# Attention, routed experts and a second network on one core: the cross products of split operands go from float32r to bfloat16

## The chip, the cores and the metric

The kernel runs on one core of one Trainium2 chip. Its time is the time on the device, in microseconds (us), from launch to end; 825.88 us is the median of three executions before the change. Less is better.

## The reference

Three stages feed each other. Everything is float32 at the interface.

```python
# 1. attention over B, H, S, D = 4, 8, 576, 64, plus a memory term
a = softmax(q @ k.T / 8, causal);  local = a @ v
mem = (phi(q) @ M_prev) / (phi(q) @ z_prev + 1e-6)      # phi(x) = max(x, 0) + exp(min(x, 0))
x = (sig(beta) * mem + (1 - sig(beta)) * local)         # 2304 tokens of 512
# 2. routing: each token goes to one of 8 experts, 288 tokens each, greedily by score
order = argsort(-(x @ w_gate).flatten())                # first come, first served
out[tokens of e] = maximum(x[tokens of e] @ w1[e], 0) @ w2[e]       # 512 -> 1024 -> 512
# 3. the second network, on all tokens
h = maximum(maximum(x @ w1, x @ w2), x @ w3);  y = h @ w_out        # 512 -> 768 -> 512
```

## The kernel before

**Attention** (`attention`) works through 16 pairs of heads. While it runs, 24 tiles of the second network's weights are loaded and turned into float32, and the first four of twelve blocks of 1024 columns are split in two parts (lines 976 to 995). It ends with the gate's scores in `L` and the 2304 rows of x in DRAM.

**Routing** (`routing`) takes eight rounds, one per expert. A round finds the expert that fills next by a search with thresholds: VectorE writes 0/1 flags into a tile `cq` (line 1140), TensorE counts them with tiny bfloat16 matmuls (line 1148), VectorE narrows the interval, and so on. Then VectorE and TensorE turn the round's 288 tokens into a list of indices (lines 1211 to 1225): `cq` holds one-hot rows of 96 columns, and line 1219 uses all its 128 columns as weights. Columns 32 to 127 of `cq` are set to zero once by GpSimd (line 1062), since the first round fills only part of them. The first round is the only one with nothing else to do on TensorE; 88 dummy matmuls on `ones` (line 1310) are spread over its end.

**Experts and second network** (`experts`) go through the eight experts in the order in which routing finds them. For expert p: gather 288 rows of x (three indirect DMAs of GpSimd), transpose them, then for each of 8 weight blocks `fb` the first product h1 (16 groups of matmuls into the PSUM tile `w`), ReLU, and the second product y (into four PSUM tiles `acc`). The second network follows for the same 288 tokens: six feature blocks of three products each (p stage, line 1523 on), maximum over the three, and the output product o on chunks of 128 tokens, with 512 columns. So each matmul of h1, y and p moves 288 columns, and each of o moves 512.

**Split operands.** Every operand of these products is kept in two float32r parts: `hi`, the value rounded to float32r, and `lo`, what is left. The helper `mm3` issues three matmuls per product:

```python
nc.tensor.matmul(o, wh, rh, start=start, stop=False)    # line 1430
nc.tensor.matmul(o, wh, rl, start=False, stop=False)    # line 1431
nc.tensor.matmul(o, wl, rh, start=False, stop=stop)     # line 1432
```

ScalarE makes `hi` (lines 1282, 1321, 1377 and the helper `copy`, line 1268), VectorE makes `lo` by a subtraction (lines 1295, 1327, 1329, 1383). `W32` are the second network's float32 weights, `mh` and `ml` their parts, `wraw`, `whi`, `wlo` those of an expert, `hh` and `hl` the hidden layer's, `gf`/`gc` the maximum's. Blocks 4 and 5 of `ml` are made by another way: ScalarE writes minus `mh`, and a DMA adds `W32` to it (lines 1286 and 1289).

**What sets the order.** Each engine executes its instructions in one fixed order. `Plan` builds that order when the kernel is built: a task has a key (due time), a cost per engine and dependencies, and a list scheduler places them. Keys and costs are the numbers in `RKEY`, `R1KEY`, `FK` and in the `add` calls. So a changed key moves instructions on all engines.

Of the kernel before, what the change touches and what calls it, by code (L numbers as in the profile page):

```python
# [17 lines left out]
try:  # L18
# [4 lines left out]
F32 = mybir.dt.float32  # L23
# [22 lines left out]
RKEY = (-1000, -66.2)  # L46
FL0 = 3
NFILL = 88
R1, R1KEY = 9, 28.8
NK, KD = 4, 6  # L50
# [4 lines left out]
         "mt": 2, "ob": 3, "gc": 7, "gf": 2}  # L55
FK = {"m2": -600, "ml": 28.3, "load": -59.9, "w2": -3.8, "wsplit": -31.9, "gather": -128.4, "xt": -126.2, "h1": 0, "y": 4.0, "o": 12.0, "store": 68.8, "idx": -41.0}
# [185 lines left out]
def attention(g, tc, ctx, consts, beta, qN, kN, v1, vT, mz, mT, wg, xd, L, m2):  # L242
# [738 lines left out]
    for k in range(NK):  # L981
# [6 lines left out]
        def fl(e, k=k, a=0):  # L988
            if a == 0:
                g.slot(k)  # L990
            V.tensor_sub(g.ML[k][:, a:a + 512], g.W32[k][:, a:a + 512], g.MH[k][:, a:a + 512].bitcast(F32))
# [3 lines left out]
        low = add(n + .2, {"DVE": dve(512)}, lambda e, fl=fl: fl(e, a=512), [low])  # L995
    emit(tc, plan)
# [45 lines left out]
def routing(g, tc, plan, rt, rps, L):  # L1042
# [19 lines left out]
    plan.op(-600, {"POOL": 800}, lambda e: nc.gpsimd.memset(cq[:, :, 32:], 0.0), (), [f"cq{a}" for a in range(0, NB, CQ[0])])  # L1062
# [59 lines left out]
    for ph in range(E):  # L1122
# [87 lines left out]
        for a in range(0, NB, q):  # L1210
# [6 lines left out]
            def idx(a0=a + q - w, w=w):  # L1217
# [3 lines left out]
            r.ti = P((30 if ph else 70) * w + (60 if ph else 0), idx, " ".join(f"cq{x}" for x in range(a + q - w, a + q, q)) + " mov0 mov1 mov2" +  # L1221
# [26 lines left out]
def experts(g, tc, plan, top, wr, xd, idxd, out):  # L1248
# [12 lines left out]
    def act(n):  # L1261
        return 35 + 0.89 * n
# [13 lines left out]
    def msub(t, i, c, n):  # L1276
        return t[3 * i + c // 1024][:, c % 1024:c % 1024 + n]

    low = None
    for k in range(NK, 12):  # L1280
# [3 lines left out]
        def fneg(e, k=k):  # L1284
            g.slot(k)
            A.mul(ML[k], MH[k].bitcast(F32), -1.0)

        def facc(e, k=k):
            G.dma_start(ML[k].bitcast(F32), g.W32[k], accum_op=OP.add)

        def flow(e, k=k, h=0):
# [3 lines left out]
            V.tensor_sub(ML[k][:, q], g.W32[k][:, q], MH[k][:, q].bitcast(F32))  # L1295
# [403 lines left out]
```

## Time and profile before

| what | value |
|---|---|
| median of three executions | 825.88 us (824.94 to 826.33) |
| the profiled execution, its own time | 824.29 us |
| its span, first to last instruction | 822.2 us |
| granted TensorE clock, mean of the span | 0.981 of 2.4 GHz |
| TensorE busy | 789.6 us, 96% |
| VectorE, ScalarE, GpSimd busy | 560.3, 355.9, 109.0 us |
| attention, about | 0 to 242 us |
| first routing round and first gather, about | 242 to 276 us |
| experts and second network, about | 276 to 815 us |

The profiled execution is 1.59 us below the median of the three. Matmuls are pipelined, and the record of one is much longer than the distance to the next; so the distance between the starts of two matmuls is read, not the length of a record. The same holds on the other engines, to a lesser degree.

### The profile page before, as it was taken

How to read it: one execution, taken by the hardware profiler on the slowest of the kernel's cores; microseconds unless marked ns; L12 is line 12 of the kernel's file. 1: busy time of each engine (PE TensorE's matmuls, PEld its weight loads, DVE VectorE, ACT ScalarE, POOL GpSimd, SP SyncE). 2: the span in 40 equal slices, each digit the busy share in tenths (PEclk: the TensorE clock that was granted, in tenths of full speed). 3: DMA queues.
4: the chain of work that ended last, by engine and by line, in shares of the span. 5: the costliest groups of instructions: out<-in, count | busy, mean ns of one | idle time of the engine just before them, and what ended most of it. 6: DMA issues, size and time to landing. Idle time of an engine off the chain costs nothing.

```text
span 822.2 us, 18334 instructions
## 1 busy us (share of the span) xinstructions
PE 789.6 (96%) x7022; PEld 745.9 (91%) x7022; DVE 560.3 (68%) x1687; ACT 355.9 (43%) x941; POOL 109.0 (13%) x242
## 2 busy tenths in 40 slices
PE   8999999999974899999999999999999999999996
PEld 6898999999974899999999999989999999999995
DVE  7799999999456996896677576575667643533321
ACT  4668776767645431344234235224313423423311
POOL 2212222223112100301020011011002011001001
PEclk9999999999995899999999999999999999999999
DMA  8364747565015412344033015004303621521000
GB/s 243 90 222 144 242 125 246 165 208 165 23 59 103 146 53 78 119 129 145 2 108 127 27 43 192 27 14 157 103 2 109 138 44 66 142 24 52 1 2 39
DMA packets 39534, 84.82 MB, mean 103 GB/s; under 512 B 11486, under 2 KB 14230, under 8 KB 39446
## 3 DMA queue, kind: packets, MB, share of 16 engines
q1 hardware_dynamic: 35574, 72.87, 29.0%
q0 software_dynamic: 3872, 10.78, 4.6%
q8 instruction: 55, 0.90, 0.5%
q14 instruction: 33, 0.27, 0.1%
HBM read 72.77 MB, written 9.74 MB: 100 GB/s over the span
## 4 chain that ended last, share of the span: by engine, by line
PE 77%; issue 11%; DVE 7%; DMA 2%; POOL 1%; ACT 1%; SPq 0%; DVEq 0%; POOLq 0%; ACTq 0%
PE w L1430 12%; PE w L1431 12%; PE w L1432 12%; PE av L684 9%; PE acc L1430 6%; PE acc L1431 6%; PE acc L1432 6%; PE st L643 5%; PE rps L590 2%; PE rps L1148 2%; DVE junk L456 2%; PE rps L543 1%; PE w L1407 1%; PE st L443 1%; DMA QN<-in_qN 1%
## 5 line engine op out<-in xcount | busy, mean ns | idle before, releaser
L1430 PE MATMUL w<-yh,mh 128*128 128x288 f32 x576 | 172.1, 299 | 0.0
L1431 PE MATMUL w<-yl,mh 128*128 128x288 f32 x576 | 170.3, 296 | 0.0
L1432 PE MATMUL w<-yh,ml 128*128 128x288 f32 x576 | 169.5, 294 | 0.0
L1431 PEld LDWEIGHTS w<-yl,mh 128*128 128x128 f32 x576 | 108.3, 188 | 1.8
L1430 PEld LDWEIGHTS w<-yh,mh 128*128 128x128 f32 x576 | 108.2, 188 | 1.9
L1432 PEld LDWEIGHTS w<-yh,ml 128*128 128x128 f32 x576 | 108.3, 188 | 0.0
L684 PE MATMUL av<-V,pt 128*128 128x112 f32 (+1 forms) x960 | 105.3, 261 | 1.7 <-issue 0.6
L684 PEld LDWEIGHTS av<-V,pt 128*128 128x128 f32 (+1 forms) x960 | 97.0, 173 | 6.4 <-issue 2.3
L1383 DVE TENSOR_TENSOR wlo<-wraw,whi 128x512 fp32r<-128x512 f32 x128 | 84.3, 685 | 13.7 <-ACT whi L1377 13.5
L1537 DVE TENSOR_TENSOR mt<-w,mt 128x288 f32<-128x288 f32 x96 | 43.7, 455 | 61.7 <-PE w L1432 61.1
L1377 ACT CAST whi<-wraw 128x512 fp32r<-128x512 f32 x128 | 73.2, 620 | 21.8 <-DMA wraw<-in_wr 11.4
L1430 PE MATMUL w<-xhi,whi 128*128 128x288 f32 x256 | 77.3, 302 | 0.7 <-DVE xlo L1329 0.7
L1268 ACT CAST gc<-mt 128x64 fp32r<-128x64 f32 (+2 forms) x72 | 17.4, 245 | 138.3 <-DVE mt L1537 111.4
L1430 PE MATMUL acc<-hh,whi 128*128 128x288 f32 x256 | 76.5, 299 | 0.0
L1431 PE MATMUL w<-xlo,whi 128*128 128x288 f32 x256 | 76.1, 297 | 0.0
L1432 PE MATMUL w<-xhi,wlo 128*128 128x288 f32 x256 | 75.9, 296 | 0.0
L1431 PE MATMUL acc<-hl,whi 128*128 128x288 f32 x256 | 75.4, 294 | 0.0
L1432 PE MATMUL acc<-hh,wlo 128*128 128x288 f32 x256 | 75.1, 293 | 0.0
L456 DVE CUSTOM_DVE_ANT_0 junk<-st,mask 128x512 bf16<-128x512 f32 (+3 forms) x128 | 62.5, 488 | 15.6 <-ACT pt L668 4.0
L1321 ACT ACTIVATE hh<-w 128x288 fp32r<-128x288 f32 x64 | 26.3, 411 | 92.9 <-PE w L1432 87.1
L1327 DVE SCALAR_TENSOR_TENSOR hl<-w,hh 128x288 fp32r<-128x288 f32 x64 | 29.1, 455 | 47.3 <-ACT hh L1321 46.7
L670 ACT ACTIVATE pt<-st 128x512 f32<-128x512 f32 x96 | 53.3, 601 | 16.2 <-PE st L643 15.9
(272 smaller groups left out, 1706.7 us busy)
## 6 DMA issues: line engine op xcount, KB each, us to landing
wraw<-in_wr SPq DMA_DIRECT2D x64, 512.0 KB, 3.8
m2raw<-in_m2w SPq DMA_DIRECT2D x12, 512.0 KB, 5.5
V<-in_v SPq DMA_DIRECT2D x16, 365.0 KB, 4.9
KR<-in_kN SPq DMA_DIRECT2D x16, 288.0 KB, 3.1
QN<-in_qN SPq DMA_DIRECT2D x16, 288.0 KB, 3.3
vt<-in_vT SPq DMA_DIRECT2D x16, 288.0 KB, 5.3
xd<-x SPq DMA_DIRECT2D x16, 256.0 KB, 2.9
m2raw<-in_m2w SPq DMA_DIRECT2D x12, 256.0 KB, 3.2
```

The source lines that it names most:

```text
L456: V.tensor_tensor_reduce(out=junk[:, :w], in0=o.s[x][:, c:c + w], in1=m, scale=1.0, scalar=-3.0e38, op0=OP.add, op1=OP.max, accum_out=r.nm ...
L643: PE.matmul(d[:kr, c:c + z - a], neg[q, :kr] if wt is None else wt[q, k], mv[q, a:z], start=x == 0, stop=x == 3)
L670: A.activation(r.PT[:, i, 512 * gi:512 * gi + 512], o.t[i], AF.Exp, scale=0.125)
L684: PE.matmul(AV[:m, i, j * C:j * C + w], r.PT[:, i, o:o + m], r.V[:, c:c + w], start=kb == 0, stop=kb == j)
L1321: A.activation(hi(), src(), AF.Relu)
L1327: V.scalar_tensor_tensor(lo(), src(), 0.0, hi().bitcast(F32), op0=OP.max, op1=OP.subtract)
L1377: A.copy(x.W[fb][0][:, q], x.RAW[fb][:, q])
L1383: V.tensor_sub(x.W[fb][1][:, q], x.RAW[fb][:, q], x.W[fb][0][:, q].bitcast(F32))
L1430: nc.tensor.matmul(o, wh, rh, start=start, stop=False)
L1431: nc.tensor.matmul(o, wh, rl, start=False, stop=False)
L1432: nc.tensor.matmul(o, wl, rh, start=False, stop=stop)
L1537: V.tensor_max(q.mt, o.pt[:, :T], q.mt)
```

## The change

1. **The two cross products on bfloat16.** `lo` becomes a bfloat16 tile with two planes: plane 0 is the rest as before, rounded to bfloat16, and plane 1 is `hi` rounded to bfloat16. `mm3` keeps the first matmul in float32r and does the other two on bfloat16 parts. The tiles have the same size in bytes.
2. **One more instruction per split** makes plane 1: on ScalarE for weights (`wlo`, `ml`), on ScalarE or VectorE for the rest, as the scheduler finds better. `hi` of an operand that isn't ReLU may now also be made by VectorE.
3. **Finer tasks where stages change**: the last block of y and the first product of p are two tasks each, first the float32r matmuls, then the bfloat16 ones.
4. **No clearing of `cq`** (line 1062 is gone); line 1219 in the first round uses 96 of its columns instead of 128.
5. **Blocks 4 and 5 of `ml`** are made like the others; the two DMAs go.
6. New keys and costs.

```diff
-RKEY = (-1000, -66.2)
+RKEY = (-1000, -23.5)
-R1, R1KEY = 9, 28.8
-NK, KD = 4, 6
+R1, R1KEY = 9, 21.8
+NK = 4
...
         low = add(n + .2, {"DVE": dve(512)}, lambda e, fl=fl: fl(e, a=512), [low])
+        low = add(n + .3, {"ACT": act(1024)}, lambda e, k=k: A.copy(g.ML[k][:, 1], g.MH[k].bitcast(F32)), [low])
...
-    plan.op(-600, {"POOL": 800}, lambda e: nc.gpsimd.memset(cq[:, :, 32:], 0.0), (), [f"cq{a}" for a in range(0, NB, CQ[0])])
...
-                    nc.tensor.matmul(IX, cq[:, x], mov[:, x], start=(x == 0), stop=(x == NB - 1))
+                    nc.tensor.matmul(IX[:z], cq[:, x, :z], mov[:, x], start=(x == 0), stop=(x == NB - 1))
...
-        if k < KD:
-            low = add(FK["m2"] + k + .1, {"ACT": act(1024)}, fneg, [t, low])
-            low = add(FK["m2"] + k + .2, {"POOL": 1100}, facc, [low], lat=11000)
-        else:
-            for h in range(2):
-                low = add(FK["ml"] + .1 * k + .05 * h, {"DVE": dve(512)}, lambda e, f=flow, h=h: f(e, h=h), [t, low, g.rounds[0].tt])
+        for h in range(2):
+            low = add(FK["ml"] + .1 * k + .05 * h, {"DVE": dve(512)}, lambda e, f=flow, h=h: f(e, h=h), [t, low, g.rounds[0].tt])
+        low = add(FK["ml"] + .1 * k + .07, {"ACT": act(1024)}, lambda e, k=k: A.copy(ML[k][:, 1], MH[k].bitcast(F32)), [low])
...
-        t = add(key, {"ACT": act(n)}, f1, dep, new=new, use=use)
-        return t, add(key + .01, {"DVE": dve(n)}, f2, [t] + list(dep), use=list(new) + list(use))
+        t = add(key, {"ACT": act(n)} if relu else {"ACT": act(n), "DVE": dve(n)}, f1, dep, new=new, use=use)
+        t2 = add(key + .01, {"DVE": dve(n)}, f2, [t] + list(dep), use=new + use)
+        return t, t2, add(key + .02, {"ACT": act(n), "DVE": 60 + 0.8 * n}, lambda e: copy(e, lo(1), hi().bitcast(F32)), [t], use=new + use)
...
-                    x.W[fb][1] = st("wlo", [128, 1024], F32R)
+                    x.W[fb][1] = st("wlo", [128, 2, 1024], BF)
...
+            def fhb(e, x=x, fb=fb, h=0):
+                q = slice(512 * h, 512 * h + 512)
+                A.copy(x.W[fb][1][:, 1, q], x.W[fb][0][:, q].bitcast(F32))
...
-        def mm3(o, wh, wl, rh, rl, start, stop):
-            nc.tensor.matmul(o, wh, rh, start=start, stop=False)
-            nc.tensor.matmul(o, wh, rl, start=False, stop=False)
-            nc.tensor.matmul(o, wl, rh, start=False, stop=stop)
+        def mm3(o, w, r, start, stop, part=(0, 1)):
+            if 0 in part:
+                nc.tensor.matmul(o, w[0], r[0], start=start, stop=False)
+            if 1 in part:
+                nc.tensor.matmul(o, w[2], r[1], start=False, stop=False)
+                nc.tensor.matmul(o, w[1], r[2], start=False, stop=stop)
```

**Where instructions move: VectorE, start of the first routing round.** `cq` are the flags, `m` the best score of each token, `kst` the thresholds. Before, from the last scores to the first count:

```order
L1097 TENSOR_REDUCE m<-L 128x6 [waits DVE_49]
L1098 TENSOR_TENSOR e_4068<-L,m 128x48 [waits DVE_49]
L1140 TENSOR_TENSOR cq<-m,kst 128x384 [waits Pool_49]
L1099 TENSOR_TENSOR e_4068<-e_4068,w_3284 128x48 [waits DVE_49]
L1140 TENSOR_TENSOR cq<-m,kst 128x384
```

The same place after the change:

```order
L1097 TENSOR_REDUCE m<-L 128x6 [waits DVE_49]
L1098 TENSOR_TENSOR e_4072<-L,m 128x48 [waits DVE_49]
L1140 TENSOR_TENSOR cq<-m,kst 128x384
L1099 TENSOR_TENSOR e_4072<-e_4072,w_3288 128x48 [waits DVE_49]
L1140 TENSOR_TENSOR cq<-m,kst 128x384
```

Only the wait for GpSimd on the third row is gone; the order is the same.

**ScalarE, between the hidden blocks of an expert in the middle of the program.** `hh` is the ReLU, `whi` the rounding of a half block of weights. Before:

```order
L1321 ACTIVATE hh<-w 128x288 [waits DVE_49,PE_49]
L1377 CAST whi<-wraw 128x512 [waits DMAHW7_49,PE_49]
L1377 CAST whi<-wraw 128x512
L1321 ACTIVATE hh<-w 128x288 [waits DVE_49,PE_49]
L1377 CAST whi<-wraw 128x512 [waits DMAHW0_49,PE_49]
```

And after the change:

```order
L1313 ACTIVATE hh<-w 128x288 [waits PE_49]
L1380 CAST wlo<-whi 128x512 [waits Activation_49]
L1268 CAST hl<-hh 128x288 [waits Activation_49]
L1380 CAST wlo<-whi 128x512
L1370 CAST whi<-wraw 128x512 [waits DMAHW2_49,PE_49]
L1370 CAST whi<-wraw 128x512
L1313 ACTIVATE hh<-w 128x288 [waits DVE_49,PE_49]
L1380 CAST wlo<-whi 128x512 [waits Activation_49]
L1268 CAST hl<-hh 128x288 [waits Activation_49]
```

Between two `hh` there are now two casts of 512, two more of 512 and one of 288, where two of 512 were.

**TensorE, a group of h1 and the y that follows, after the change** (before, each group is three float32r rows L1430, L1431, L1432 without rows for the weights):

```order
L1429 MATMUL w<-xhi,whi 128x288
L1431 LDWEIGHTS wlo
L1431 MATMUL w<-xlo,wlo 128x288
L1432 LDWEIGHTS wlo
L1432 MATMUL w<-xlo,wlo 128x288
L1429 MATMUL acc<-hh,whi 128x288 [waits Activation_49]
L1431 LDWEIGHTS wlo
L1431 MATMUL acc<-hl,wlo 128x288 [waits DVE_49]
L1432 LDWEIGHTS wlo
L1432 MATMUL acc<-hl,wlo 128x288 [waits Activation_49]
```

A float32r matmul and two bfloat16 matmuls now alternate, and the third of a y group waits for ScalarE's second plane.

## Rows read from the trace of the kernel before

**Rows 1.** Windows: length, PE, PEld, DVE, ACT, POOL busy (x), clock, DMA, GB/s.

```profile
0.00:230.00 230.00, 223.18 (x2394) 203.67 (x2394) 195.36 (x636) 157.41 (x452) 56.09 (x174) 1.00 0.54 168
230.00:276.00 46.00, 27.89 (x353) 25.15 (x351) 31.07 (x130) 20.41 (x55) 10.25 (x11) 0.74 0.40 103
410.00:480.00 70.00, 70.00 (x581) 66.69 (x581) 48.97 (x138) 23.45 (x61) 5.53 (x7) 1.00 0.24 77
...
286.00:296.00 10.00, 10.00 (x92) 9.93 (x89) 9.97 (x22) 3.56 (x8) 0.00 (x0) 1.00 0.33 108
```

**Rows 2.** Groups by line and shape, TensorE, 276 to 822 us: busy us, mean ns.

```profile
L1431 PE MATMUL w<-yl,mh 128*128 128x288 f32 x576 | 170.3, 296 | 0.0
L1431 PE MATMUL w<-xlo,whi 128*128 128x288 f32 x256 | 76.1, 297 | 0.0
L1431 PE MATMUL acc<-hl,whi 128*128 128x288 f32 x256 | 75.4, 294 | 0.0
L1431 PE MATMUL acc<-ml,gf 128*128 128x512 f32 x72 | 28.3, 392 | 0.0
L1431 PE MATMUL acc<-ml,gc 128*128 128x512 f32 x36 | 14.2, 394 | 0.0
```

**Rows 3.** Timeline, TensorE, 560 to 566 us: start us, us, what.

```profile
559.71 0.30 PE L1430 MATMUL acc<-hh,whi 128*128 128x288 f32 x1
...
565.90 0.29 PE L1432 MATMUL acc<-hh,wlo 128*128 128x288 f32 x1
```

**Rows 4.** Timeline, TensorE, the last 512-column matmuls.

```profile
808.84 0.39 PE L1430 MATMUL acc<-mh,gc 128*128 128x512 f32 x1
...
814.81 0.40 PE L1432 MATMUL acc<-mh,gf 128*128 128x512 f32 x1
```

**Rows 5.** Timeline, TensorE, bfloat16 matmuls of 256 columns at the start.

```profile
14.39 0.27 PE L812 MATMUL av<-warm 128*128 128x256 bf16 x1
...
15.77 1.47 PE L812 MATMUL av<-warm 128*128 128x256 bf16 x12 [0.26 <-ACT nm L523]
```

**Rows 6.** Timeline and window (busy, clock, DMA), TensorE, the first expert's first matmuls.

```profile
277.40 0.44 PE L1430 MATMUL w<-xhi,whi 128*128 128x288 f32 x1
...
278.84 0.44 PE L1430 MATMUL w<-xhi,whi 128*128 128x288 f32 x1
...
276.00:278.00 2.00, 1.48 (x6) 0.50 0.74 227
```

**Rows 7.** Timeline, TensorE and its weight loads, after tiny bfloat16 matmuls.

```profile
335.61 0.17 PE L1158 MATMUL rps<-fl,ones 128*128 128x8 bf16 x1
335.62 0.19 PEld L1430 LDWEIGHTS acc<-mh,gf 128*128 128x128 f32 x1
335.64 0.48 PE L1430 MATMUL acc<-mh,gf 128*128 128x512 f32 x1
335.72 0.19 PEld L1431 LDWEIGHTS acc<-ml,gf 128*128 128x128 f32 x1
...
335.96 0.40 PE L1431 MATMUL acc<-ml,gf 128*128 128x512 f32 x1
```

**Rows 8.** Timeline, start of the first routing round: ScalarE, GpSimd, VectorE.

```profile
244.97 0.39 ACT L1110 ACTIVATE kst<-iota_row,st 128x32 bf16<-128x32 f32 x1
...
246.61 2.42 POOL L1062 MEMSET cq<- 128x1728 bf16 x1
...
249.06 0.56 DVE L1140 TENSOR_TENSOR cq<-m,kst 128x384 bf16<-128x384 f32 x1 [5.39 <-POOL cq L1062]
```

**Rows 9.** Timeline, TensorE, counts of the first round: 128 and 64 columns of weights.

```profile
250.62 0.30 PE L1148 MATMUL rps<-ohU,cq 128*128 128x8 bf16 x6 [7.82 <-DVE ohU L1101]
...
259.64 1.42 PE L1148 MATMUL rps<-ohU,cq 128*64 128x8 bf16 x18 [1.26 <-DVE cq L1140]
```

**Rows 10.** Timeline, ScalarE: casts of 1024 and of 512 columns.

```profile
249.11 5.81 ACT L1282 CAST mh<-w 128x1024 fp32r<-128x1024 f32 x6
...
330.92 2.18 ACT L1377 CAST whi<-wraw 128x512 fp32r<-128x512 f32 x4
```

More of the change, by code (lines that the diff above doesn't have):

```diff
@@ L1317, in split @@
     def split(key, n, src, hi, lo, dep, new=(), use=(), relu=False):
+        new, use = list(new), list(use)
         def f1(e):
@@ L1473, in experts, with fy @@
             for hf, (fb, ts, o, bhh, bhl) in itertools.product(range(2), yt):
-                def fy(e, x=x, fb=fb, hf=hf, o=o):
+                def fy(e, x=x, fb=fb, hf=hf, o=o, part=(0, 1)):
                     for d in (2 * hf, 2 * hf + 1):
@@ L1490, in hi @@
                 if not hasattr(x, "yh"):
-                    x.yh, x.yl = st("yh", [128, 4, T], F32R), st("yl", [128, 4, T], F32R)
+                    x.yh, x.yl = st("yh", [128, 4, T], F32R), st("yl", [128, 2, 4, T], BF)
                 return x.yh[:, d]
-            x.ty += list(split(k0 + 18 + .1 * d, T, lambda x=x, d=d: x.acc[d][:, :T], hi, lambda x=x, d=d: x.yl[:, d],
-                               [ylast[-3 + d // 2 * 2]] + x.ty[:1], new=x.by if d == 0 else [], use=[ya[d]] + ([] if d == 0 else x.by)))
+            x.ty += list(split(k0 + 18 + .1 * d, T, lambda x=x, d=d: x.acc[d][:, :T], hi, lambda i, x=x, d=d: x.yl[:, i, d],
+                               [ylast[-4 + d // 2 * 3]] + x.ty[:1], new=x.by if d == 0 else [], use=[ya[d]] + ([] if d == 0 else x.by)))
         chunks = range(p * T // 128, (p + 1) * T // 128)
@@ L1520, in experts, with fp @@
                 for hf in range(2):
-                    def fp(e, x=x, f=f, i=i, hf=hf, o=o):
-                        if hf == 0:
+                    def fp(e, x=x, f=f, i=i, hf=hf, o=o, part=(0, 1)):
+                        if hf == 0 and 0 in part:
                             o.pt = ps.tile([128, 512], F32, name="w", bufs=FBUFS["w"])
@@ L1525, in fp @@
                             s = slice(d * F2 + f * 128, d * F2 + f * 128 + 128)
-                            mm3(o.pt[:, :T], msub(MH, i, s.start, 128), msub(ML, i, s.start, 128), x.yh[:, d], x.yl[:, d], d == 0, d == 3)
-                    need = x.ty[:4] if hf == 0 else x.ty + [t]
-                    t = tp = add(kf + i + .1 * hf, {"PE": 800}, fp, need + TM[i], new=[bp] if hf == 0 else [],
-                            use=([] if hf == 0 else [bp]) + x.by)
+                            mm3(o.pt[:, :T], msub(i, s.start, 128), tri(x.yh, x.yl, d), d == 0, d == 3, part)
+                    for part in ((0,), (1,)) if f == 0 and i == 0 else ((0, 1),):
+                        need = x.ty[:6] if hf == 0 else x.ty + [t]
+                        if part == (0,):
+                            need = x.ty[6 * hf:6 * hf + 6:3] + ([t] if hf else [])
+                        elif part == (1,):
+                            need = need + [t]
+                        t = tp = add(kf + i + .1 * hf + .05 * part[0], {"PE": 270 * (0 in part) + 490 * (1 in part)},
+                                     lambda e, f=fp, part=part: f(e, part=part), need + TM[i], new=[bp] if hf == 0 and 0 in part else [],
+                                     use=([] if hf == 0 and 0 in part else [bp]) + x.by)
                 def fm(e, i=i, o=o, q=q):
```

72 lines of the change are left out of this document (38 added, 34 removed).

## The prediction

> **What bounds the kernel now.** I read the windows first, to find which stage is limited by what, then the groups of matmuls by shape, then the timeline of TensorE at places where nothing disturbs it, and last the start of the first routing round. In the windows [rows 1] the reader is to see three stages. In attention TensorE, VectorE and ScalarE are all well used (157.41 us of 230 on ScalarE). From 230 to 276 us TensorE is busy for 27.89 us of 46 and its clock is at 0.74 on average: here the work hangs on a chain through VectorE, GpSimd and tiny counts. In the stretch from 410 to 480 us TensorE is busy throughout at full clock, VectorE for 48.97 us of 70 and ScalarE for 23.45. So from 276 us on, what TensorE takes per matmul is what the kernel takes; the two others have room, except in the first expert, where VectorE shows 9.97 us of 10 (286 to 296 us).
>
> A busy TensorE says nothing about its pace, so I take distances between starts. From 559.71 to 565.90 us there are 48 matmuls of 288 columns and no gap [rows 3]: 6.19 / 47 = **0.1317 us** each. From 808.84 to 814.81 us, 27 of 512 columns [rows 4]: 5.97 / 26 = **0.2296 us**. All of these are float32r. Right after the first routing round the same matmul of 288 columns took (278.84 - 277.40) / 6 = 0.240 us at a granted clock of 0.50, that is 1.2 GHz [rows 6]: one column per cycle. At 2.4 GHz one column per cycle would be 0.120; the row has 0.1317. So at full clock float32r doesn't keep one column per cycle. The only long run of large bfloat16 matmuls is the dummy work at the start, 256 columns with a weight load each [rows 5]: 12 of them take 1.47 us and one record is 0.27 long, so (1.47 - 0.27) / 11 = **0.1091 us**, against 0.1067 for one column per cycle. Bfloat16 keeps that pace.
>
> **The two cross products.** Lines 1431 and 1432 have 576 + 256 + 256 = 1088 matmuls of 288 columns each and 72 + 36 = 108 of 512 (the rows of line 1431 are shown [rows 2], those of 1432 have the same counts). From the 256-column row I take 0.1091 x 288 / 256 = 0.1227 us and 0.1091 x 2 = 0.2182 us. That saves 2 x 1088 x (0.1317 - 0.1227) = 19.6 us and 2 x 108 x (0.2296 - 0.2182) = 2.5 us, together **22.1 us**, all on the path. The bounds: with exactly one column per cycle 29 us. At the other end, one of the two cross products could be held at 0.1317 by the float32r weights that load behind it, which leaves 11 us.
>
> Behind a matmul, the next weights load. After tiny bfloat16 matmuls, which last 0.03 us (335.61 to 335.64), nothing hides that load [rows 7]: the load of line 1430's weights starts at 335.62, the next at 335.72, and the matmul between them reaches 335.96, 0.32 us after its start instead of 0.23. So a float32r load takes 0.10 us, and a bfloat16 matmul of 0.1227 us should hide it, with 0.02 us to spare. I count no cost, but this is the narrowest cover in the sum, and two rivals rest on it.
>
> The Trainium skill weighs against the whole term: its page "TensorE: Matmul & The Clock Gate", section "Back-to-back issue gap", gives N / 2.4 + 2.5 ns between warm matmuls and no dependence on the type. The trace agrees for bfloat16 (109.2 ns by the rule at 256 columns), but not for float32r (122.5 ns by the rule at 288, 131.7 in the rows). By the rule alone this part would save nothing.
>
> The weight loads of bfloat16 are instructions of their own on TensorE, 2392 more. The 12 matmuls at 0.1091 us have them too [rows 5], and six counts with a load each took 0.30 us [rows 9], so issuing them is not a limit.
>
> **No clearing of cq.** The first flags of the first round start at 249.06 us on VectorE after 5.39 us of idling, released by GpSimd's clearing, which ran from 246.61 to 249.03 behind that engine's DMA issues [rows 8]. Without it the same instruction has no wait and can follow at 243.67. What is late next is ScalarE's first set of thresholds (244.97 to 245.36 [rows 8]), which only the second set of flags wants, after a count and three small steps. So all 5.39 us should go; the least is 0, if another wait stands there. Against it, the round's 18 index matmuls now use 96 columns of weights. Counts with 64 columns took 1.42 / 18 = 0.079 us and with 128 columns 0.30 / 6 = 0.050 [rows 9]; no row has 96, so I take 1.5 times the former, 0.118 (bounds: 0.050, as for 128, and 0.158, twice that of 64). That is 18 x 0.068 = 1.2 us on the path, less some 0.3 us for dummy matmuls that no longer stand between them: +0.9 us. Net **-4.5 us**.
>
> **What the second plane costs.** ScalarE gets 128 casts of 512 columns for expert weights, 12 of 1024 and some 250 smaller ones, a few of which go to VectorE. Casts of 512 go at 2.18 / 4 = 0.545 us, of 1024 at 5.81 / 6 = 0.97 [rows 10]. Three places matter.
> - Attention: four of the 12 run there. ScalarE is 68% busy, so most fit in gaps; 0 to 3.9 us, I take **+0.5**, since the chain at the end of attention is mostly TensorE's.
> - First expert: VectorE is the tight engine [rows 1], and four subtractions come to it from the DMA way of blocks 4 and 5. They are at most 0.75 us each (0.56 for 384 columns in rows 8). And a faster TensorE gains nothing there: 128 cross products x 0.009 = 1.2 us. Bounds 0 to 4.2, I take **+1.5**.
> - Hidden layer of every expert: per weight block TensorE now takes 8 x (0.1317 + 2 x 0.1227) = 3.02 us, and ScalarE 4 x 0.545 plus 2 x 0.31 = 2.80 us, where it had 1.40. It fits, at 93%, in blocks whose weights aren't split beforehand. y's third matmul waits for ScalarE's plane, and all of TensorE's queue waits behind it. I take **+1.0** over the eight experts; the bounds are 0 and the rival below.
>
> The new keys reorder the weight loads and the later rounds; the same 64 loads stay hidden behind the blocks multiplied meanwhile (DMA share 0.24 [rows 1]; a late one would cost its lateness), two DMAs leave GpSimd's queue, the gathers stay on it, and the finer tasks at the stage changes move no cost: TensorE has no gap there now.
>
> **Sum.** -22.1 - 4.5 + 0.5 + 1.5 + 1.0 = -23.6 us. The profiled execution took 824.29 us, which gives 800.7; it stands 1.59 below the median of three, so I forecast a median of **802.3 us**.
>
> **Rivals.**
> 1. *The float32r load isn't quite hidden.* The matmul before it stays at 0.1317, so half of the 22.1 us go: 813.4. For it: 0.02 us to spare is little. Against it: at 512 columns, with all that time to hide the load, float32r is slow just the same (0.2296 against 0.2133), so its pace is set by its columns. 13%.
> 2. *ScalarE's queue makes TensorE wait.* An `hh` that arrives behind a cast of 512 waits up to 0.545 us, and between h1 and its y stand as few as 12 matmuls, 1.5 us, for `hh` and `hl` in turn. At 0.15 us in each of 64 blocks that is 9.6 us: 811.9. For it: 93%. Against it: four blocks can be split ahead. 14%.
> 3. *Slower.* If TensorE can't load float32r weights behind a bfloat16 matmul at all, every triple pays what the rows show after counts, 0.09 to 0.10 us: 1196 x 0.095 = 114 us, so about 916. It decides from 0.02 us per triple (23.6 / 1196). For it: each such change of type in the trace has that penalty. Against it: the matmuls ahead were 0.03 us long [rows 7], so they couldn't hide the load. 4%.
> 4. *The type doesn't matter*, as the page's rule has it: 0.1317 comes from something that all such chains share. Then only the first round gains: 802.3 + 22.1 = 824.4. Against it: rows 5. 4%.
>
> **The numbers.** My forecast has 65%, with a range of its own of 797 to 808. Rivals 1 and 2 bring the upper end to 813.5; below 797 the sum would need nearly one column per cycle and no new stall. About 0.2% (1.7 us) can be told from no change: faster has the forecast and rivals 1 and 2, 0.92; same has rival 4, 0.04; slower has rival 3, 0.04.
>
> **What would show it.** Right: starts at 0.132, 0.123, 0.123 us in a triple; the first flags near 243.7 us and the first expert some 4.5 us earlier; no more than a few us of gaps behind ScalarE, whose busy time rises by some 150 us. Wrong: triples longer than 0.395 us (rival 3), or of three nearly equal steps (rivals 1 and 4), or TensorE idle behind `hh`, `hl` or `wlo` in each block (rival 2).

## The result, and the profile after

| | before | after |
|---|---|---|
| median | 825.99 us of 4 (824.94 to 826.33) | 816.44 us of 4 (814.94 to 816.85) |
| ratio, 95% interval | | 0.9883, 0.9866 to 0.9900 |
| span of the profiled execution | 822.2 us | 814.6 us |
| TensorE busy | 789.6 us | 783.8 us |
| VectorE, ScalarE, GpSimd busy | 560.3, 355.9, 109.0 us | 578.6, 480.7, 107.6 us |

The change is faster by 9.6 us, not by the 23.6 that I forecast, and its time lies outside my range (797 to 813.5).

The windows of the changed kernel, over two of the stretches of [rows 1] and one more (length, then busy time and count of PE, PEld, DVE, ACT, POOL, then the granted clock, the DMA share and GB/s):

```profile
410.00:480.00 70.00, 70.00 (x602) 52.54 (x601) 49.21 (x149) 39.63 (x100) 9.41 (x10) 1.00 0.24 81
286.00:296.00 10.00, 8.05 (x75) 5.98 (x73) 8.29 (x14) 7.70 (x16) 0.00 (x0) 1.00 0.60 103
295.00:300.00 5.00, 4.60 (x24) 3.29 (x24) 4.67 (x10) 5.00 (x11) 0.00 (x0) 0.66 0.00 0
```

In the long stretch from 410 us TensorE is still busy throughout, ScalarE has risen from 23.45 to 39.63 us, and TensorE issues 602 matmuls where it issued 581, only 3.6% more. In the first expert (286 to 296) it is now idle for 2 us of 10, and just after that the clock is at 0.66; before it was busy throughout [rows 1].

The timeline of TensorE in the long stretch (start us, us, what):

```profile
560.09 0.30 PE L1431 MATMUL w<-xlo,wlo 128*128 128x288 bf16 x1
560.22 0.29 PE L1432 MATMUL w<-xlo,wlo 128*128 128x288 bf16 x1
560.25 0.39 PE L1429 MATMUL w<-xhi,whi 128*128 128x288 f32 x1
560.48 0.30 PE L1431 MATMUL w<-xlo,wlo 128*128 128x288 bf16 x1
...
562.83 0.30 PE L1431 MATMUL acc<-hl,wlo 128*128 128x288 bf16 x1
```

From the first row to the last there are seven triples (a triple is the three matmuls of one product): (562.83 - 560.09) / 7 = 0.391 us, against 3 x 0.1317 = 0.395 before [rows 3]. I had forecast 0.377. From line 1431 to 1432, two bfloat16 matmuls, the step is 0.13 us, not 0.123. The start of a float32r record (line 1429) says little: it begins 0.03 us after the one before it and is 0.39 long, so it holds a wait, and triples are read from line 1431 to line 1431.

The first routing round, in VectorE's timeline, against [rows 8]:

```profile
243.35 0.21 DVE L1098 TENSOR_TENSOR e<-L,m 128x48 f32<-128x48 f32 x1
243.48 0.55 DVE L1140 TENSOR_TENSOR cq<-m,kst 128x384 bf16<-128x384 f32 x1
```

The first flags come at 243.48 without a wait (forecast 243.67, before 249.06). The first expert's first product starts at 272.50 us, where it started at 276.52: 4.0 of the 4.5 us that I forecast. But the second network's first product, which ends the first expert's stretch, starts at 305.58 us against 305.04 before. So the first expert loses again what the round gained: 33.1 us from its first matmul to there, where it took 28.5. TensorE's timeline shows where:

```profile
293.41 0.40 PE L1429 MATMUL w<-xhi,whi 128*128 128x288 f32 x1
295.40 0.30 PE L1431 MATMUL w<-xlo,wlo 128*128 128x288 bf16 x1 [1.59 <-ACT wlo L1380]
...
296.60 0.46 PE L1431 MATMUL w<-xlo,wlo 128*128 128x288 bf16 x1
...
297.35 0.46 PE L1431 MATMUL acc<-hl,wlo 128*128 128x288 bf16 x1
```

TensorE stands still for 1.6 us, and a microsecond after it runs again its clock falls: the granted clock is 0.66 on average from 295 to 300 us, and a triple takes 0.75 us (296.60 to 297.35), as at 1.2 GHz. The five triples to 299.9 cost another 1.6 us. The wait is put down to ScalarE's second plane `wlo`; SyncE's queue (SPq), and the chain of work that ended last, lead one step further back:

```profile
279.27 0.33 SPq L1361 DMA_DIRECT2D wraw<-in_wr  x1
279.66 0.43 SPq L1512 DMA_DIRECT2D idxd<-tidx  x1
282.56 0.35 SPq L1361 DMA_DIRECT2D wraw<-in_wr  x1
288.93 0.40 SPq L1516 DMA_DIRECT2D idx<-idxd  x1
```

```profile
282.56 10.16 DMA wraw<-in_wr
```

The seventh weight block is asked for at 282.56 us, behind the write of the index list (`idxd`), and needs 10.16 us to land, where a block takes 4.3 by the median of this profile. A list ahead of a block is not new: before, the same list was written at 279.84, and the seventh block was asked for only when the list had been read back:

```profile
279.84 0.42 SPq L1503 DMA_DIRECT2D idxd<-tidx  x1
288.61 0.41 SPq L1507 DMA_DIRECT2D idx<-idxd  x1
289.62 2.92 SPq L1368 DMA_DIRECT2D wraw<-in_wr  x2
```

```profile
294.58 1.15 ACT L1377 CAST whi<-wraw 128x512 fp32r<-128x512 f32 x2 [0.41 <-DMA wraw<-in_wr]
```

There ScalarE had it 5.0 us after it was asked for, 18.1 after the first matmul (276.52); in the change it has it 20.2 after (292.74, first matmul 272.50), although it asked for it 3 us earlier, counted in the same way. So what is new is a block that is asked for while the list is under way. From 305.58 us on the change takes 501.4 us to its last matmul and the kernel before 509.8: 8.3 us less, which is what the faster cross products left there, net of the new order.

So two questions went to the chip: why a triple takes 0.391 and not 0.377 us, and what makes the first expert lose its lead.

### The profile page after: what moved, and what is told of

It reads as the page before. It is cut to its first block, busy times and chain, and to the rows that moved or that the text cites. A ratio compares the mean times of both kernels' runs of the same rounds, so it can differ in the third digit from the quotient of the medians.

```text
span 814.6 us, 18746 instructions
## 1 busy us (share of the span) xinstructions
PE 783.8 (96%) x7022; PEld 623.4 (77%) x7022; DVE 578.6 (71%) x1780; ACT 480.7 (59%) x1238; POOL 107.6 (13%) x239
## 4 chain that ended last, share of the span: by engine, by line
PE 73%; issue 9%; DVE 8%; DMA 5%; ACT 3%; POOL 1%; SPq 1%; DVEq 0%; POOLq 0%; ACTq 0%
PE w L1431 12%; PE w L1429 12%; PE w L1432 11%; PE av L684 9%; PE acc L1429 6%; PE acc L1431 6%; PE acc L1432 5%; PE st L643 5%; PE rps L590 2%; PE rps L1148 2%; PE rps L543 1%; DMA wraw<-in_wr 1%; DVE junk L456 1%; DMA m2raw<-in_m2w 1%; PE w L1405 1%
## 5 line engine op out<-in xcount | busy, mean ns | idle before, releaser
L1429 PE MATMUL w<-yh,mh 128*128 128x288 f32 x576 | 219.8, 390 | 0.2 <-DVE mt L1552 0.2
L1431 PE MATMUL w<-yl,ml 128*128 128x288 bf16 x576 | 169.4, 296 | 0.0
L1432 PE MATMUL w<-yl,ml 128*128 128x288 bf16 x576 | 163.7, 286 | 0.0
L1429 PEld LDWEIGHTS w<-yh,mh 128*128 128x128 f32 x576 | 107.6, 190 | 17.9 <-DVE mt L1552 0.6
L1429 PE MATMUL w<-xhi,whi 128*128 128x288 f32 x256 | 100.3, 392 | 0.5 <-DVE xlo L1321 0.5
L1376 DVE TENSOR_TENSOR wlo<-wraw,whi 128x512 bf16<-128x512 f32 x128 | 84.2, 686 | 15.2 <-ACT whi L1370 14.4
L1431 PEld LDWEIGHTS <-ml 128*128 128x128 bf16 x576 | 55.0, 96 | 39.0 <-issue 7.2
L1431 PE MATMUL w<-xlo,wlo 128*128 128x288 bf16 x256 | 76.8, 300 | 1.9 <-ACT wlo L1380 1.9
L1380 ACT CAST wlo<-whi 128x512 bf16<-128x512 f32 x128 | 76.2, 616 | 0.0
L1431 PEld LDWEIGHTS <-wlo 128*128 128x128 bf16 x512 | 49.4, 96 | 34.4 <-ACT wlo L1380 2.4
L1431 PE MATMUL acc<-hl,wlo 128*128 128x288 bf16 x256 | 75.7, 298 | 0.0
L1432 PE MATMUL w<-xlo,wlo 128*128 128x288 bf16 x256 | 74.0, 289 | 0.0
L1432 PE MATMUL acc<-hl,wlo 128*128 128x288 bf16 x256 | 73.1, 288 | 0.1
L1345 POOL DMA_INDIRECT xg<-xd,tidx x24 | 30.1, 1253 | 255.7 <-PE w L1432 233.3
L1432 PEld LDWEIGHTS <-ml 128*128 128x128 bf16 x576 | 57.1, 99 | 0.6
```

Of the source, the lines that this page charges most:

```text
L1345: g.gather = G.indirect_dma_start(out=x.xg[:96, c], out_offset=None, in_=xd, in_offset=bass.IndirectOffsetOnAxis(ap=r.tidx[:96, c:c + 1], ...
L1376: V.tensor_sub(x.W[fb][1][:, 0, q], x.RAW[fb][:, q], x.W[fb][0][:, q].bitcast(F32))
L1380: A.copy(x.W[fb][1][:, 1, q], x.W[fb][0][:, q].bitcast(F32))
L1429: nc.tensor.matmul(o, w[0], r[0], start=start, stop=False)
L1431: nc.tensor.matmul(o, w[2], r[1], start=False, stop=False)
L1432: nc.tensor.matmul(o, w[1], r[2], start=False, stop=stop)
```

## The experiments

Each time stands beside the kernel before on the same chip, 825.1 to 825.7 us; the change's ratio, to compare with, is 0.9883. The edits are abridged; `...` marks what is left out.

### 1. Streams of matmuls by themselves

```diff
+for i in range(96):  # bf16: zeros / data / a new weight tile each / summed by twelve
+    mm(pt[:, :288], w(bh[0], i), mv(bh[1], i, 288), start=..., stop=...)
+# then float32r alone and summed, "fbb" triples, of zeros, two and four triples by type; 512 columns
```

> A kernel of its own that leaves the whole computation of the reference out: it loads three weight blocks, warms TensorE and then issues streams of 48 to 96 matmuls back to back; nothing else runs beside them. Read is the pitch (last start less first start, by the count). The question is why the change's matmuls of 288 columns follow one another by 0.130 us (0.391 a triple) where the prediction took 0.1227 for a bfloat16 one. Theory A (accumulation): a bfloat16 matmul alone, start and stop both set, has 0.123; summed by twelve into one bank it has about 0.130, as float32r has 0.132 alone or summed. Theory B (the float32r weight load, or the change of type, holds each triple up by some 0.013 to 0.02): bfloat16 summed is still 0.123, float32r 0.132 and the triple 0.391 where 0.377 would be the sum of its parts; grouping by type (two or four triples at once) gives 0.384 and 0.380 a triple. Theory C (data, power or a new weight tile each time): zeros with one weight tile 0.123, data or new tiles 0.130, without accumulation too; the triple of zeros is at 0.377. Theory D (contention with the other engines' traffic): all bfloat16 streams here are at 0.123 and the triple at 0.377, since nothing runs beside them.

The timeline (at 288 columns, the next bfloat16 group's start ends a bfloat16 stream; the row at 149.89 begins with that stream's second matmul, since the record of a float32r matmul behind a bfloat16 one starts early):

```profile
17.26 11.93 PE L81 MATMUL p<-zb 128*128 128x288 bf16 x96
29.02 11.92 PE L84 MATMUL p<-bh,bh 128*128 128x288 bf16 x96
40.78 11.92 PE L87 MATMUL p<-bh,bh 128*128 128x288 bf16 x96
52.54 11.92 PE L90 MATMUL p<-bh,bh 128*128 128x288 bf16 x96
64.20 13.05 PE L93 MATMUL p<-hi,hi 128*128 128x288 f32 x96
77.09 12.96 PE L96 MATMUL p<-hi,hi 128*128 128x288 f32 x96
89.89 0.29 PE L103 MATMUL p<-hi,hi 128*128 128x288 f32 x1
90.02 0.42 PE L103 MATMUL p<-bh,bh 128*128 128x288 bf16 x2
90.18 0.39 PE L103 MATMUL p<-hi,hi 128*128 128x288 f32 x1
...
102.28 0.39 PE L103 MATMUL p<-zr 128*128 128x288 f32 x1
...
115.11 0.67 PE L103 MATMUL p<-bh,bh 128*128 128x288 bf16 x4
...
126.61 0.67 PE L103 MATMUL p<-bh,bh 128*128 128x288 bf16 x4
...
127.64 1.15 PE L103 MATMUL p<-bh,bh 128*128 128x288 bf16 x8
...
138.30 1.16 PE L103 MATMUL p<-bh,bh 128*128 128x288 bf16 x8
139.30 10.52 PE L115 MATMUL p<-bh,bh 128*128 128x512 bf16 x48
...
149.89 10.98 PE L117 MATMUL p<-hi,hi 128*128 128x512 f32 x47
...
182.62 0.58 PE L103 MATMUL p<-hi,hi 128*128 128x512 f32 x1
183.04 0.61 PE L103 MATMUL p<-bh,bh 128*128 128x512 bf16 x2
...
192.11 0.58 PE L103 MATMUL p<-hi,hi 128*128 128x512 f32 x1
```

Bfloat16 takes 0.1225 us (11.76 / 96), with zeros or data, one weight tile or many, alone or summed: the 0.1227 of my prediction is right for such a stream, and theories A and C fall. Float32r takes 0.133. But a triple takes (102.28 - 90.18) / 31 = 0.390, where its parts give 0.133 + 2 x 0.1225 = 0.378. Nothing else ran here, so theory D falls too, and 0.012 us a triple belongs to the alternation of the types (theory B). At 512 columns a record of a bfloat16 matmul is 0.38 us long and one of float32r 0.39, so the parts are (10.52 - 0.38) / 47 = 0.216 and (10.98 - 0.39) / 46 = 0.230, together 0.662, and a triple takes 9.49 / 14 = 0.678: 0.016 more. The step from the first bfloat16 matmul behind a float32r one to the second is 0.132 at 288 columns and 0.226 at 512 (means over the streams; 0.42 less a record of 0.29, and 0.61 less 0.38, in the rows), so most of the loss lies in that first one.

In pairs by type (two float32r matmuls, then four bfloat16 ones) a triple takes (126.61 - 115.11) / 15 / 2 = 0.383, in fours (138.30 - 127.64) / 7 / 4 = 0.381. A pair is 0.010 us above the sum of its parts and a four is too, about as much as a single triple: the loss comes once per return to bfloat16, whether one, two or four float32r matmuls and weight loads stand before. So it goes with the change of type; what in the change costs it stays open.

### 2. and 3. One type for all three products, in the kernel

```diff
-nc.tensor.matmul(o, w[2], r[1], ...); nc.tensor.matmul(o, w[1], r[2], ...)
+nc.tensor.matmul(o, w[0], r[0], ...)   # three times: float32r
+nc.tensor.matmul(o, w[2], r[2], ...)   # the main product, in the other kernel: bfloat16
```

> The changed kernel with float32r in all three products of every triple (the high parts three times, so the low parts are left out of the products); every other engine has the same instructions. If the cross products gained what the prediction took (22 us), this is 22 slower than the change, near 838. By the triples of the changed kernel's trace (0.391 against 0.395 and 0.681 against 0.689) it is 6 to 8 slower, near 823, and the cross products' term was the one that failed, mis-sized by a factor of three.

Measured: 826.34 us, ratio 1.0014 (1.0005 to 1.0023). The cross products give about 10 us (826.34 - 816.44) in the change's own order, not 22.1, and a little more than the 6 to 8 that I expected.

> The changed kernel with bfloat16 in all three products of every triple (the main product too, which costs its precision), the first products of the split tasks moved behind their split point. Theory A (a bfloat16 matmul that accumulates takes 0.130 by itself): triple 0.39, time within 4 us of the change. Theory B (the float32r load or the change of type holds a bfloat16 triple up): triple 0.368, 1088 x 0.023 = 25 us faster than the change, near 791. Theory D (contention): triple 0.385 to 0.39 as under A, but the streams of the kernel by itself are at 0.123.

Measured: 786.15 us, ratio 0.9527 (0.9513 to 0.9540), 30 us faster than the change: theory B, and by more than I expected of it, since the 25 us left out the 108 triples of 512 columns (0.680 by the mean in the change, 0.647 here: 3.5 us). The triple in its timeline:

```profile
560.01 0.29 PE L1431 MATMUL w<-yl,ml 128*128 128x288 bf16 x1
560.14 0.29 PE L1432 MATMUL w<-yl,ml 128*128 128x288 bf16 x1
560.26 0.29 PE L1430 MATMUL w<-yl,ml 128*128 128x288 bf16 x1
560.38 0.29 PE L1431 MATMUL w<-yl,ml 128*128 128x288 bf16 x1
...
561.12 0.29 PE L1431 MATMUL w<-yl,ml 128*128 128x288 bf16 x1
```

(561.12 - 560.01) / 3 = 0.37 us, by the mean of some 900 undisturbed triples 0.367 = 3 x 0.1225 (undisturbed: nothing between their matmuls, and none at the lower clock). So in the full kernel, with all its traffic, bfloat16 keeps the stream's pace as soon as no float32r matmul stands between.

### 4. and 5. The clearing, put back and taken out alone

```diff
 cq = tl("cq", [NB, 128], BF)
+plan.op(-600, {"POOL": 800}, lambda e: nc.gpsimd.memset(cq[:, :, 32:], 0.0), ...)   # run 4, in the change
-plan.op(-600, {"POOL": 800}, lambda e: nc.gpsimd.memset(cq[:, :, 32:], 0.0), ...)   # run 5, in the kernel before
```

> The changed kernel with the clearing of cq put back on POOL and all 128 columns in the first round's index matmuls. The prediction took 4.5 us for this part (5.4 of wait less 0.9), and the change's trace has its first expert 4.0 us earlier. If the head's gain is kept to the end: 3.5 to 5 us slower than the change, near 820.5. If it is lost again in the first expert (which now has 4.7 us of gaps where 0.8 were), it is 0 to 1.5 slower.

> The kernel before with the clearing of cq left out and the first round's index matmuls on 96 columns; types, casts and the experts' tasks as before. If the 5.4 us of waiting that go are passed on to the end, as the prediction took it: 4.5 to 5.5 faster than the kernel before, near 820.5. If the first expert cannot use an earlier start, because its weight blocks arrive no earlier (the other reading of the 4.7 us of gaps in the change's first expert): 0 to 2 faster, and the gaps show here too, without a single added cast.

Both runs also set the index matmuls of the first round (128 columns in run 4, 96 in run 5), which the cut leaves out. Run 4: 823.56 us, ratio 0.998 (0.9971 to 0.9989), 7.1 slower than the change and more than I expected: its first expert starts 5.3 us later (277.81) and takes 34.9 us, 1.8 more than in the change. Of runs with the change's order for this expert, run 14 takes 34.2 and run 17 33.6, so I don't count the 1.8 to the clearing. Run 5: 819.87 us, ratio 0.9944 (0.9930 to 0.9957), 5.2 faster than before; its first expert starts 5.45 us earlier than before (271.07 us) and takes 29.0 us, without a gap. The head's gain is real and reaches the end, and an early start alone makes no gaps: both second readings fall.

### 6. Triples grouped by type

```diff
-for d in pair: mm3(..., (0, 1))
+for q in range(2):
+    for d in pair: mm3(..., (q,))     # both float32r, then the four bfloat16
```

> The changed kernel with the triples of a task taken two by two: both float32r products first, then the four bfloat16 ones, in the hidden layer, its second product and the second network's first three products (1088 triples, minus the two split tasks); the sums are the same. Theory B, which the streams support (0.390 a triple one by one, 0.383 in pairs, where nothing else runs): 1088 x 0.0075 = 8 us faster than the change, near 808.5. If the change of type costs nothing in the kernel and the bfloat16 products are slow there for another reason: within 1.5 us of the change.

Measured: 811.4 us, ratio 0.9834 (0.9821 to 0.9848): 5 us faster than the change. The direction holds and the size is about half to two thirds of the 8 expected (by the two ratios it is 4 us). The profiled execution was the lowest of six (807.34, the others 810.6 to 812.1), so its trace doesn't show what the rest lost.

### 7. to 10. The added casts

```diff
-return t, t2, add(key + .02, {"ACT": ..., "DVE": ...}, lambda e: copy(e, lo(1), hi().bitcast(F32)), ...)
+return t, t2, t2                                                   # runs 7 and 8: re-planned
+return t, t2, add(key + .02, {...}, lambda e: None, ...)           # runs 9 and 10: counted, not emitted
```

> The changed kernel with float32r operands throughout, low parts too, as the kernel before has them, so that all added casts on ScalarE go; the task tables, the finer tasks and the missing clearing stay as in the change. Beside the run with float32r in all products (826.3, casts kept) it differs by the casts alone. If ScalarE's casts make the first expert wait for its weight parts (rival 2 of the prediction, in one stage): 4 to 5 us less, near 822, and the first expert from its first matmul to the second network's first takes 28.5 to 29.5 where the change has 33.1. If the weights' arrival or the new order makes the gaps: 825 to 826.5 and the gaps stay.

> The changed kernel with high and low parts both bfloat16: high is the bfloat16 rounding, low the bfloat16 rounding of what is left, and the three products read these two parts, so that no second copy of the high part is needed and all added casts go. Triples at 0.3675 as in the run with bfloat16 in all products (786.2). If the casts make the first expert wait: 5 to 6 us less than that, near 780.5; if the weights' arrival does, near 786. In both cases it would be faster than both kernels.

Both missed: 829.42 us (1.0057, 1.0043 to 1.0071) and 789.51 (0.9564, 0.9551 to 0.9577), 3 us slower than runs 2 and 3, which have the casts. Without the casts' costs the planner makes another order, and in run 7 the stretch after the first expert is 4.6 us longer (515.7 against 511.1 from the second network's first product to the last matmul). So these two price an order, not the casts.

> As the run of float32r without casts, but every engine's instructions stay in the changed kernel's order: the planner still counts the added casts, and none is emitted. The earlier run without casts re-planned the whole order, and its later experts were longer, so it could not price the casts. Against the run with float32r in all products (826.3) only ScalarE's 200-odd casts (and VectorE's few) are gone. If the casts cost what the first expert shows (33.1 us from its first matmul to the second network's first, 28.5 before): 821.5 to 823, with that stretch near 29. If the new order is what costs it: within 1 us of 826.3 and the stretch at 32 or more.

> High and low parts both bfloat16, no added casts, and every engine in the changed kernel's order. Against the run with bfloat16 in all products and the casts kept (786.2, stretch of the first expert 33.8): if the casts cost it, 4 to 6 us less, near 781.5; if the order does, 785 to 787.

Run 9: 826.26 us, ratio 1.0007 (0.9998 to 1.0016), the same as with the casts, and the first expert still takes 33.3 us. ScalarE's timeline there:

```profile
294.95 1.14 ACT L1370 CAST whi<-wraw 128x512 fp32r<-128x512 f32 x2 [5.39 <-DMA wraw<-in_wr]
```

So with float32r the casts (373 instructions fewer on ScalarE than in the change) cost nothing and don't make the gap: without them ScalarE idles for 5.39 us, until the weight block has landed. Run 10: 782.31 us, ratio 0.9483 (0.9470 to 0.9495), 3.8 less than with the casts (786.15, run 3): with bfloat16 throughout they cost something, or the high parts do, which run 3 keeps in float32r and casts. By the two traces it is spread: 1.3 us at the first expert's start, 1.6 in its stretch, 1.0 behind it. No run takes the casts alone out of the change itself.

### 11. and 12. More buffers, and the old order with bfloat16

```diff
-FBUFS = {"wraw": 3, ...
+FBUFS = {"wraw": 5, ...         # run 11, on run 10
```

> The same with five buffers for raw weight blocks in place of three (the bfloat16 parts leave the room), so that all eight blocks of the first expert are asked for before the index list is written; the planner re-plans with five. If the first expert waits for blocks 6 and 7, whose load is issued behind a released buffer (282.6 us, landed 10.2 us later, in the change): 2 to 4 us less than with three buffers. If it waits for ScalarE or VectorE: the same within 1 us.

> The kernel before without the clearing, with its own tables and tasks, and with high and low parts both bfloat16 (the two blocks whose low part came by an accumulating DMA get it on VectorE). Against the same with float32r (819.9): 1088 x (0.3970 - 0.3675) = 32 and 108 x (0.691 - 0.648) = 4.6, together 37, near 783 if nothing else becomes the bound. Near 781 or under, with the first expert's stretch at 28 or less, speaks for the change's order or finer tasks as a cost of their own; 785 and over for them as a gain.

Run 11: 782.87 us (0.9476, 0.9461 to 0.9492). The first expert takes 25.7 us in place of 32.1, so it was the blocks that it waited for; but the total is the same as run 10's, because the re-planned second and third experts are 2.7 and 4.2 us longer. Run 12 (all edits of run 8 in the kernel before): 788.53 us (0.9557, 0.9544 to 0.9569), 31 us less than with float32r where I expected 37, and 6 slower than run 10, which has the same types in the new order. By my own reading (785 and over) that speaks for the new order as a gain; but the second expert takes 71.1 us, 9 more than in run 10, and I didn't follow why. So run 12 says nothing clean about the order.

### 13. and 15. What makes the seventh block late

```diff
-t = add(k0 + FK["idx"], {"SP": 500}, fi, [r.tt] + x.tl[FL0:FL0 + 1], lat=2300)
+t = add(k0 + FK["idx"], {"SP": 500}, fi, [r.tt] + (x.tl[FL0:FL0 + 1] if p else x.tl[7:]), lat=2300)   # run 13
-FK = {..., "w2": 17.1, "wsplit": -3.5, ...
+FK = {..., "w2": -3.8, "wsplit": -31.9, ...                                                          # run 15
```

> The changed kernel with one dependency changed: the first expert's index list is written and read back after its eighth weight block is asked for, not after the sixth and seventh; four rows move on SyncE's queue, nothing on any other engine. In the change the seventh block is asked for at 282.6 us, behind the list, and lands 10.2 us later, where a block takes 4.5 by the median. If that makes the gap: it lands by 288, the gap of 2.0 us at 293 goes and with it the half clock from 296.4 to 299.9 (1.75 us): 3 to 4 us faster than the change, ratio to before near 0.984. If another engine's order makes it: within 0.8 us of the change.

Measured: 814.27 us, ratio 0.9861 (0.9847 to 0.9876), 2.2 less than the change, where I expected 3 to 4; the two intervals overlap, so the size rests on the trace as well. SyncE's queue and the window after the former gap:

```profile
283.73 3.77 SPq L1361 DMA_DIRECT2D wraw<-in_wr  x2
287.55 0.43 SPq L1512 DMA_DIRECT2D idxd<-tidx  x1
296.93 0.41 SPq L1516 DMA_DIRECT2D idx<-idxd  x1
```

```profile
295.00:300.00 5.00, 5.00 (x41) 3.86 (x40) 5.00 (x10) 3.99 (x9) 0.00 (x0) 1.00 0.02 0
```

The list still takes 9.4 us to its read-back, but nothing waits behind it; the gap is gone, TensorE is busy from 295 to 300 us and its clock stays at full. The first expert takes 30.6 us instead of 33.1; with bfloat16, 28.2 in runs 16 and 18 instead of 32.1 in run 10. So the list under way in front of the block is shown as a cause of 2.5 us; the other 2 us against before stay open. It is no matter of the first expert alone. A block of the last expert of the kernel before is asked for behind a list too:

```profile
713.32 0.59 SPq L1503 DMA_DIRECT2D idxd<-tidx  x1
715.60 0.33 SPq L1368 DMA_DIRECT2D wraw<-in_wr  x1
```

It lands 11.4 us after it was asked for, the slowest of the sixteen blocks whose landing that trace has; the same block of the change (list 708.19, block 710.54) takes 10.0.

> The changed kernel with the two keys that order the splitting of weight blocks as before (w2 -3.8, wsplit -31.9); the planner re-plans. If the late second halves on VectorE hold the third raw buffer (the sixth block is asked for 6.8 us after the first expert's first matmul, 2.9 before): that is near 3 again and the first expert's stretch goes from 33.1 to 29 to 31, time 2 to 4 us less than the change unless later experts lose it again. If the stretch stays at 33, the keys are not the cause.

Measured: 819.50 us (0.9927, 0.9915 to 0.9940), 3 slower than the change. The sixth block is asked for 5.3 us after the first matmul, not 3; the stretch is 32.3. These two keys alone are not the cause.

### 14. and 17. The longer gather

The first expert's start is 11.1 us behind the first index matmul, before it was 9.5. GpSimd's timeline has part of it, here of the change and, below, of the kernel before:

```profile
263.62 2.35 POOL L1345 DMA_INDIRECT xg<-xd,tidx  x1 [16.24 <-DVE R L1245]
```

```profile
257.46 0.85 POOL L1289 DMA_DIRECT2D ml<-w  x1 [7.01 <-ACT ml L1286]
269.12 1.04 POOL L1352 DMA_INDIRECT xg<-xd,tidx  x1 [10.81 <-DVE R L1245]
```

The first indirect DMA takes 2.35 us where it took 1.04, and the accumulating DMAs that made blocks 4 and 5 of `ml` no longer stand ahead of it.

```diff
+G.dma_start(pa, pb, accum_op=OP.add)                           # run 14: waits for nothing
+G.dma_start(pa[:, :1], r.e.bitcast(F32), accum_op=OP.add)      # run 17: waits for the expert's number
```

> The changed kernel with two small memsets and one small accumulating DMA on GpSimd between its last store of the attention and the first row gather, where the kernel before had its last accumulating DMA at 257.5 us. If the gather's 2.35 us (1.04 before) come from the 16 us without such work on GpSimd: the first gather is back near 1.0, and the time 1.0 to 1.3 us less than the change. If not: the gather stays at 2.3 and the time within 0.5 us.

> The changed kernel with one small accumulating DMA on GpSimd that waits for the first expert's number (about 257 us), 5 us before the first row gather. If a DMA issued shortly before keeps the gather short: 1.0 to 1.1 us in place of 2.35, the first expert starts 1.3 us earlier, time 1.0 to 1.5 us less than the change. If not (the gather is short for another reason): 2.3 again, time within 0.6 us.

Run 14's DMA had nothing to wait for and ran 15.8 us ahead of the gather: 818.26 us (0.9910, 0.9895 to 0.9925), 1.8 slower than the change, the gather at 2.33. Run 17 puts it at the right time:

```profile
258.07 0.90 POOL L1351 DMA_DIRECT2D pwa<-ei  x1 [10.14 <-DVE g L1185]
264.33 2.33 POOL L1345 DMA_INDIRECT xg<-xd,tidx  x1 [5.36 <-DVE R L1245]
```

815.66 us (0.9876, 0.9861 to 0.9891), the same as the change, and the gather is as long. My explanation falls; the cause of these 1.3 us stays open.

### 16. and 18. Joined

> High and low parts both bfloat16 in the changed kernel's order (782.5), with the index list behind the eighth block and the small DMA on GpSimd. If both reasons hold: 3 to 5 us less, near 778.

> High and low parts both bfloat16 in the changed kernel's order, the index list behind the eighth block and this DMA ahead of the gather. If the gather gets shorter: 778, a microsecond less than 779.1; if not: 779.

Run 16: 779.11 us (0.9438, 0.9426 to 0.9450); run 18: 778.76 us (0.9429, 0.9416 to 0.9442), 47 us less than before and 38 less than the change. Bfloat16 for both parts (run 10) brings nearly all of it, the moved list some 3; the small DMA by itself brought nothing in runs 14 and 17.

## Why the prediction was wrong

**The step that failed is the size of the cross products**: "From the 256-column row I take 0.1091 x 288 / 256 = 0.1227 us and 0.1091 x 2 = 0.2182 us", and from it 22.1 us. The price was right for what the row showed, one type in a row: 0.1225 us in run 1 (and 0.216 at 512 columns), and in the kernel in run 3. It didn't hold for a sequence that changes its type: the bfloat16 matmul right behind a float32r one keeps nearly float32r's pace (0.132 us where float32r takes 0.133, run 1). Of the 0.018 us per triple that I forecast the change keeps 0.006 against run 2 (0.397 less 0.391, the means of undisturbed triples), at 512 columns 0.016 (0.696 less 0.680). By these means that is 1088 x 0.006 + 108 x 0.016 = 8.3 us; by the two times it is 10, and the difference stays open.

**Rival 1** had the size (half of the term, 11 us) and not the place. I let the matmul *ahead* of the float32r load stay slow, for lack of cover, and spoke against it with the 512 columns, where a load has time to hide. That argument met the load, not the change of type: with 512 columns the loss is no smaller (0.016 against 0.012 us a triple). The sign I gave, three nearly equal steps, came as far as it can be read: the step between the two bfloat16 matmuls is 0.13, and the other two are 0.26 together.

**Rival 2** (ScalarE's queue) falls: ScalarE's busy time rose by 125 us, TensorE's waits on it from 276 to 815 us are 1.9 us in all, and with float32r the time without the casts is the same (run 9). The +0.5 and +1.0 that I put on casts were 0 there and at most 3.8 with bfloat16 (run 10); the change, whose triples lie between, has no such run.

**Rivals 3 and 4** fall: the undisturbed triple is shorter than before (0.391 against 0.397), and the type matters, by 0.011 us at 288 columns in run 1. The rule of the Trainium skill that I weighed (page "TensorE: Matmul & The Clock Gate", section "Back-to-back issue gap") gives 122.5 ns for 288 columns; that is what the bfloat16 stream shows, and not what float32r or a mixed sequence shows.

**The clearing** was right: 4.5 forecast, 5.2 in run 5, by the mechanism named: the first flags come at 243.54 there, 5.5 us earlier, and the first expert starts 5.45 earlier. The +0.9 that I took off for index matmuls with 96 columns of weights didn't come: from the first of them to the first gather's issue it is 2.14 us before (266.98 to 269.12) and 2.04 in run 5 (261.38 to 263.42). In the change the first expert starts only 4.0 us earlier, because of the longer gather.

**The new order** I costed at nothing, with "the same 64 loads stay hidden". That is the second error. Same types, no casts, no clearing: 819.87 us in the old order (run 5), 826.26 in the new one (run 9), so the order, the finer tasks and the split of blocks 4 and 5 cost 6.4 us together. In the two traces 1.8 us of it lie ahead of the first expert's first matmul (271.07 and 272.91), 4.3 in its stretch (29.0 and 33.3), 1.2 behind. Run 13 shows a third of it: one weight block, asked for while a list of 288 single words was under way. My +1.5 for the first expert named VectorE; it lost 4.6. The 6.4 is a price with float32r; with bfloat16 runs 10 and 12 have it the other way, and the change itself was not taken in the old order.

The sum with the measured terms: -10 for the types, -5.2 for the clearing, 0 for the casts, +6.4 for the order, together -8.8; measured -9.6. The casts' and the order's terms are from float32r kernels, so that the sum comes out within a microsecond is in part luck.

## What to carry to other kernels

A pace read from a run of equal instructions is a price for a run of equal instructions: where a change makes the engine alternate, measure the alternation (a stream of 100 shows it), or choose one type throughout. High and low parts both in bfloat16 gave about four times what the mixed triple gave (run 9 to run 10, 44 us, against 10), with fewer casts; it keeps less of each operand, and no number here says what that does to the accuracy of the result. And when an order is re-made, follow each queue's first instructions one by one: here a small DMA of single words ahead of a large one cost 2 us, where 373 casts, with float32r, cost nothing that the times show.

## What the runs showed of the hardware that I had not expected

- A bfloat16 matmul behind a float32r one takes 0.132 us at 288 columns and 0.226 at 512, where in a row of its own type it takes 0.1225 and 0.216 (run 1). The loss comes once per change, whether one, two or four float32r matmuls stand before.
- 288 words of 4 bytes written from SBUF to DRAM take 9.3 us until their read-back is issued (279.66 to 288.93), and a block of 512 KB asked for 2.9 us after them lands in 10.2 us, not 4.3 (in the kernel before, one asked for 2.3 us after a list lands in 11.4).
- After TensorE stood still for 1.6 us and ran again for a microsecond, its triples took 0.75 us for 3.5 us, at a granted clock of 0.66 on average (295 to 300 us; 1.2 GHz is 0.5): with the slow triples this gap cost twice its length. Without the gap (run 13) that window has 1.00.
- The first indirect DMA after attention took 1.04 us on GpSimd in the kernel before and in run 5, 2.35 in the change and most runs of it, and 1.74 to 1.76 in runs 8, 10, 11, 12 and 16, with the same instruction each time. A small DMA ahead of it made no difference. What sets it stays open.
